# A spectral filter and a gated MLP on one core: W in six transfers, remainders on row halves, inverse tails as 32x32 blocks, and ten deferred tiles

## The chip, the cores and the metric

The kernel runs on one NeuronCore of a Trainium2 chip. The metric is device time in microseconds. The kernel before took 496.24 us (median of three runs, 496.06 to 496.64).

## What is computed

The input is one sequence of 2048 tokens with 576 features. A layer norm is filtered in two-dimensional frequency space and added to the input; a second layer norm goes through a gated MLP with 4608 hidden features and is added too.

```python
def _A_ref(x, w_r, w_i):
    X = jnp.fft.rfft2(x.astype(jnp.float32), axes=(-2, -1))
    X = X * (w_r + 1j * w_i)
    return jnp.fft.irfft2(X, s=(S, D), axes=(-2, -1)).astype(jnp.bfloat16)

def _B_ref(x, w_gate, w_up, w_down):
    return (_gelu(x @ w_gate) * (x @ w_up)) @ w_down

h = x + _A_ref(_layernorm(x), A_w_r, A_w_i)
h2 = h + _B_ref(_layernorm(h), B_w_gate, B_w_up, B_w_down)
```

`w_r` and `w_i` are 2048 x 289 each, in bf16. The transforms are done as matrix products with tables that lie in DRAM beside the inputs.

## The kernel before, in words

Sixteen tiles of 128 tokens each go through five stages. The orders of work in the first three are written out by hand in strings (`SEQ1`, `SEQF`, `SEQ`); each word is a step and its index. `Prog` turns reads and writes into semaphore waits, so each engine works through its own queue strictly in the order in which the steps were written.

**First stage (`SEQ1`, 0 to 20 us).** For each tile the statistics of the layer norm are taken on DVE (`B`) or on ACT (`S`, `Q`). Six groups of two or three tiles then get their scale (`v`, `q`, `c`), which is multiplied into the transform table `ATB` on GpSimd or DVE (`x..P`, `x..D`, result `ATS`); `n` negates half of the input on GpSimd. `M` runs the matmuls over tokens on PE (line 520), `k` runs matmuls on zeros while PE waits, and `E` brings results into `U` on ACT or DVE (line 529). `U` has five planes; plane 4 holds the 32 + 32 remainder features (256 to 287 and 544 to 575) on its rows 0 to 63. Rows 64 to 127 of it are set to zero once.

**Filter (`SEQF`, 20 to 52 us).** There are sixteen groups of frequencies. For each, `D` transforms over features (line 574: six matmuls with 128 rows, two of them on plane 4; evicted into `CUS` with a stride of two elements), `B` finishes the forward transform (line 584, into `YS`), `T` multiplies by W on DVE (line 594), `Z` adds the products into `ZS` and into the remainder `ZR` (lines 600 and 603), `V` starts the inverse over tokens (line 610, into `V`), and `R` does the same for the remainders of four groups at once (line 620), whose rows are then brought into `VR` in pieces of 32 partitions (line 565, four evictions a time). `VR` has a column for all sixteen groups, and all of it is zero but the pieces, so that the matmuls that read it can be 128 x 128.

**W.** `WS` holds three planes for each group: minus the imaginary part, the real part, the imaginary part. SyncE issues 36 transfers for it, after `VT` and before `DT`, `IT`, `DP`, `ITD` and `IDT`. The negative plane is made on GpSimd in sixteen steps (line 632), followed by the zeroing of `VR` (line 635). After these GpSimd issues the loads of the gate weights, and SyncE, after its tables, those of the up weights. The first third (slot 0) has its own place; slots 1 and 2 lie where W was.

**Inverse of the first eight tiles (`SEQ`, 52 to 65 us).** `I` is the inverse over features (line 684, six matmuls into two banks, the last of each three on `VR`), `N` the last step over tokens with the residual (lines 723 and 726), `s`, `m`, `r`, `q`, `c` and `n` the second layer norm, and `A`, `D` and `z` turn a tile on PE into `HT0` (line 777).

**MLP (65 us to the end).** There are four blocks of 512 tokens. For each, 36 chunks of 128 hidden features: eighteen matmuls with 64 rows (line 824, two row halves into two banks), GELU on ACT, a product on DVE. Then `down` (line 874): for each of the four tiles two halves of 36 matmuls. In the first block the inverse of tiles 8 to 15 (`def_i`, line 841, and `def_n`, line 855) is put into the matmuls of `down`, one in each half: `def_i` at its start, `def_n` before matmul 22. Tiles 4 to 7 are normed at chunks 15, 18, 21 and 24 of the first block and turned by DMA.

Matmuls in `def_i` before the change:

```python
for o in range(2):
    for t_ in range(2):
        for i, ch in enumerate((o, 2)):   # 128 x 144 each, ch == 2 reads VR
```

Of the kernel before, what the change touches and what calls it, by code (L numbers as in the profile page):

```python
# [10 lines left out]
KW = 288  # L11
HK = 144
NZ = 5
NVZ = 15
# [7 lines left out]
NPRE = 8  # L22
GROUPS = ((0, 2), (2, 4), (4, 7), (7, 10), (10, 13), (13, 16))
SEQ1 = """k14 B0 B1 v0 Q2 S2 B3 q0 v1 n0 n2 c0 q1 S4 x0D c1 M0 E1A B6 E0A Q4 B5 B7 x1P v2 E2D n1 B8 E3A E4A k104 M1 q2 c2 B9 Q10 E5A E7A n3 v3 S10 B12 E6A q3 c3 x2P B11 k202 M2 E9A x3P Q13 v4 E12A E8A q4 n4 B14 c4 B15 E10A E11A S13 E13D M3 E14A E15A v5 x4P E16D q5 E17A c5 E18A M4 n5 x5D E20D E19A E22D E21A M5 E23D E24A E25A E27A E26D E29A E28D""".split()
ACT_TILES = tuple(int(w[1:]) for w in SEQ1 if w[0] == "Q")
SEQF = """D0 D1 B0 D2 D3 T0 B1 D4 T1 B2 Z0 Z1 D5 T2 Z2 B3 D6 T3 B4 T4 D7 B5 Z4 D8 Z3 V0 B6 T5 Z5 T6 V1 B7 V3 Z6 T7 D9 R0 B8 D10 V2 Z7 D11 T8 B9 V6 B10 Z8 T9 R1 B11 V4 Z9 D12 D13 V5 T10 B12 T11 Z10 V7 B13 Z11 T12 T13 D14 R2 V9 D15 B14 V8 B15 Z12 V10 Z13 V13 V11 T14 Z14 V12 V14 T15a T15b Z15b Z15a R3 V15 R4""".split()
RENG = [['dve', 'dve', 'dve', 'dve'], ['dve', 'dve', 'dve', 'dve'], ['dve', 'dve', 'dve', 'act'], ['dve', 'dve', 'dve'], ['dve']]
QR = ((0, 2), (2, 4), (4, NPRE), (NPRE, 16))
SEQ = """I0 I1 N0 I2 s0 N1 I3 N2 m0 s1 I4 r0 q0 s2 N3 c0 m1 s3 n1 n0 r1 I5 q1 N4 I6 A1 c1 n3 A0 n2 N5 I7 D2 z3 N6 N7""".split()
# [11 lines left out]
def build_tables():  # L41
# [7 lines left out]
    T = {}  # L49
    n1 = np.arange(128)[:, None]  # L50
# [17 lines left out]
    I = I.reshape(4, 16, 2, 16, 128).transpose(1, 0, 2, 3, 4)  # L68
# [239 lines left out]
def _build(nc, A_x, A_w_r, A_w_i, B_w_gate, B_w_up, B_w_down, out):  # L308
# [16 lines left out]
    WS = sb.alloc("WS", [128, NG, 3, KW], BF16)  # L325
# [3 lines left out]
    VR = sb.alloc("VR", [128, NT, 2, NG, 8], BF16)  # L329
# [38 lines left out]
    FT = sb.alloc("FT", [128, 6, 2 * HK], BF16)  # L368
# [47 lines left out]
    x_load(0, 0, 2)  # L416
    x_load(1, 2, 4)
    atb_load(0, 0, 4)
    x_load(2, 4, 8)
    atb_load(1, 4, 8)  # L420
    x_load(3, 8, 12)
    x_load(4, 12, 16)
    atb_load(2, 8, 16)
    P.dma(SP, FT[:, :, :].rearrange("p a b -> p (a b)"), dram["FTAB"][:, :], "ft", w=["FT"])
    P.dma(SP, BT[:, :, :, :].rearrange("p a b c -> p (a b c)"), dram["BTAB"][:, :], "bt", w=["BT"])
    P.dma(SP, VT[:, :, :, :].rearrange("p a b c -> p (a b c)"), dram["VTAB"][:, :], "vt", w=["VT"])

    def w_loads(pl, hf, eng):
        g0, g1 = ((1, 9), (9, 16))[hf]
        src = (A_w_r, A_w_i)[pl]  # L430
        o = []
        for jj in range(4):
            o.append((WS[jj:64:4, g0:g1, 1 + pl, :], 1 + (16 * jj + g0) * K2, [[128 * K2, 16], [K2, g1 - g0], [1, K2 - 1]], jj))
            o.append((WS[64 + jj:128:4, g0:g1, 1 + pl, :], 1 + (64 + 16 * jj + 16 - g0) * K2, [[128 * K2, 16], [-K2, g1 - g0], [1, K2 - 1]], 4 + jj))
        if hf:
            for p0 in range(2):
                o.append((WS[64 * p0:64 * p0 + 64, 0, 1 + pl, :], 1 + 64 * p0 * K2, [[128 * K2, 16], [16 * K2, 4], [1, K2 - 1]], 8 + p0))
        return [lambda d=d, off=off, ap=ap, h=h: P.dma(eng, d, bass.AP(src.tensor, off, ap), f"w{pl}{hf}", w=[("W", hf, pl, h)]) for d, off, ap, h in o]

    for f in w_loads(1, 0, SP) + w_loads(1, 1, SP) + w_loads(0, 0, SP) + w_loads(0, 1, SP):  # L440
        f()
    GORD = list(range(1, NG)) + [0]
    wkeys = [[("W", hf, pl, h) for pl in range(2) for h in range(8 + 2 * hf)] for hf in range(2)]
# [6 lines left out]
    P.op(POOL, lambda g: g.memset(U[64:128, 4, :, :, :], 0.0), w=["Uz"])  # L450
# [56 lines left out]
    def a_mm(i):  # L507
        c0, c1 = GROUPS[i]
        for k in AORD:
            b = a_bank(i, k)  # L510
            for c in range(c0, c1):
                o = 128 * (c - c0)
                if k == 4:
                    parts = [(XO[:, c, 256 + 288 * h:288 + 288 * h], 32 * h, 32 * h + 32, True, True) for h in range(2)]
                else:
                    d0 = 128 * (k // 2)
                    x2 = XN[:, c, d0:d0 + 128] if k % 2 else XO[:, c, 288 + d0:416 + d0]
                    parts = [(XO[:, c, d0:d0 + 128], 0, 128, True, False), (x2, 0, 128, False, True)]
# [4 lines left out]
    def a_ev(n, eng):  # L523
        i, k = n // 5, AORD[n % 5]
        c0, c1 = GROUPS[i]
        n, b, w = c1 - c0, a_bank(i, k), 64 if k == 4 else 128
# [18 lines left out]
    P.alias([("XN", c) for c in range(NT)], [("V", g, c) for g in range(NG) for c in range(2)])  # L545
    uk = [[("U", i, k) for i in range(len(GROUPS))] + (["Uz"] if k == 4 else []) for k in range(5)]
# [4 lines left out]
    for t, w in enumerate(SEQF):  # L551
# [5 lines left out]
        elif k in "VR":  # L557
            b = min((6, 7) if ("D", LAST) not in FB else range(8), key=lambda b: used[b])
            used[b] = t + 1
        else:  # L560
            continue
# [6 lines left out]
    def st_D(i, eng=ACT):  # L568
        g = GORD[i]
        b0, s3 = FB["D", i], i % 3  # L570
        for o in range(2):
            b = b0 + o
            for m, us in enumerate((1 - o, 3 - o, 4) if o == 0 else (4, 1 - o, 3 - o)):
                P.op(PE, lambda t, b=b, m=m, us=us, o=o, g=g: t.matmul(bank(b, 0, 128, 0, 2 * HK), U[:, us, g, :, :], FT[:, 3 * o + (2 if us == 4 else us // 2), :], start=(m == 0), stop=(m == 2)),  # L574
                    r=uk[us] + ["FT"], w=[("PS", b)])
        ev(eng, CUS[:, s3, :, :].rearrange("p a (j r) -> p r a j", r=2), banks(b0, 2, 2 * HK).rearrange("p r (a j) -> p r a j", a=2),
           [("PS", b0), ("PS", b0 + 1)], [("CU", s3)])
# [10 lines left out]
    def st_T(i, q0=0, q1=KW, hs=(0, 1)):  # L588
        g, sl = GORD[i], i % 2
# [5 lines left out]
             r=[("Y", sl), ("Wn", i)] + wkeys[0 if 1 <= g < 9 else 1], w=[("T", sl, h) for h in hs])  # L595

    def st_Z(i, hs=(0, 1)):
# [3 lines left out]
        if 1 in hs:  # L601
            q, j = (i // 4 % 2, i % 4) if i < LAST else (0, 0)
# [3 lines left out]
    def st_V(i, b=6, eng=ACT):  # L606
        g, z3, sp_ = GORD[i], i % NZ, 1 if GORD[i] == 0 else 0
        for c in range(2):
            for zp in range(2):
                P.op(PE, lambda t, b=b, c=c, zp=zp, sp_=sp_, z3=z3: t.matmul(bank(b, 0, 128, 256 * c, 256 * c + 256), ZS[:, z3, zp, c:256:2], VT[:, sp_, zp, :],  # L610
                                                                            start=(zp == 0), stop=(zp == 1)), r=[("Z", z3), "VT"], w=[("PS", b)])
        for k0, k1, e in ((0, 4, eng),) if eng is not None else ((0, 2, ACT), (2, 4, ACT)):
            ev(e, V[:, :, k0:k1, g, :].rearrange("p n k e -> p k n e"), bank(b, 0, 128, 128 * k0, 128 * k1).rearrange("p (k n e) -> p k n e", k=k1 - k0, n=16),
               [("PS", b)], [("V", g, k) for k in range(k0 // 2, k1 // 2)])

    def st_R(q, engs, b=7):
        js = [i for i in range(4 * q, 4 * q + 4) if i < LAST] if q < 4 else [LAST]
        sp_, n = (1, 32) if q == 4 else (0, 32 * len(js))
        for zp in range(2):
            P.op(PE, lambda t, b=b, zp=zp, n=n, q=q, sp_=sp_: t.matmul(bank(b, 0, n, 0, 256), ZR[:, q % 2, zp, 0:n], VT[:, sp_, zp, :], start=(zp == 0), stop=(zp == 1)),  # L620
                 r=[("ZR", q % 2, j) for j in range(len(js))] + ["VT"], w=[("PS", b)])
        for j, i in enumerate(js):
            ev(engs[j], VR[32 * j:32 * j + 32, :, :, GORD[i], :].rearrange("p n k e -> p k n e"), bank(b, 32 * j, 32 * j + 32, 0, 256).rearrange("p (k n e) -> p k n e", k=2, n=16),
               [("PS", b), "Vz"], [("V", GORD[i], 2)])
# [6 lines left out]
    for i in range(NG):  # L631
        P.op(POOL, lambda v, g=GORD[i]: v.tensor_scalar(WS[:, g, 0, :], WS[:, g, 2, :], -1.0, 1.0, op0=ALU.mult, op1=ALU.mult),
             r=[k for k in wkeys[0 if 1 <= GORD[i] < 9 else 1] if k[2] == 1] + [("ATS", NT - 1)], w=[("Wn", i)])
        if i == NVZ:
            P.op(POOL, lambda g: g.memset(VR[:, :, :, :, :], 0.0), w=["Vz"])
    for w in SEQF:
        i = int(w[1:].rstrip("abc"))
        if w[0] == "D":
            st_D(i)
        elif w[0] == "B":  # L640
            st_B(i)
# [7 lines left out]
        elif w[0] == "V":  # L649
            st_V(i, FB["V", i], ACT if i < LAST else None)  # L650
# [21 lines left out]
    vk = [[("V", g, c) for g in range(NG)] for c in range(3)]  # L672
    vkeys = vk[0] + vk[1] + vk[2] + ["Vz"]
# [8 lines left out]
    def i_mm(c, h, i):  # L682
        b, kt = SLOT["I", c] + h, 2 * i + h
        P.op(PE, lambda t, b=b, h=h, i=i, kt=kt, c=c: t.matmul(bank(b, 0, 128, 0, KW), (V[:, c, kt, :, :] if kt < 4 else VR[:, c, kt - 4, :, :]), DT[:, 3 * h + i, 0:KW],  # L684
                                                              start=(i == 0), stop=(i == 2)), r=vk[i] + ["DT"], w=[("PS", b)])
# [262 lines left out]
```

## Time and profile before

| Stretch, us | what | PE busy, us | DVE busy, us | ACT busy, us | DMA share | GB/s |
|---|---|---|---|---|---|---|
| 0 to 20.0 | first stage | 16.86 | 15.37 | 15.23 | 0.81 | 248 |
| 20.0 to 27.3 | filter, before its first product | 7.04 | 0.60 | 5.52 | 0.43 | 91 |
| 27.3 to 52.4 | filter | 22.61 | 24.47 | 23.67 | 0.62 | 194 |
| 52.4 to 64.8 | inverse of eight tiles | 11.85 | 9.99 | 10.25 | 1.02 | 363 |
| 64.8 to 134.8 | chunks of block 0 | 70.00 | 27.31 | 26.92 | 0.42 | 135 |
| 134.8 to 176.2 | down of block 0 | 41.40 | 23.74 | 10.03 | 0.05 | 14 |
| 176.2 to 246.2 | chunks of block 1 | 70.00 | 27.00 | 23.71 | 0.18 | 50 |
| 246.2 to 281.6 | down of block 1 | 35.40 | 4.51 | 0.60 | 0.05 | 16 |

The profiled execution took 496.66 us; its span, from the first to the last instruction, is 494.9 us, and TensorE's granted clock was 1.00 throughout. Times in the table run from the start of the span. Busy time is the time in which at least one instruction of the engine was in flight; matmuls overlap, so a busy PE is not yet one at its limit, and starts of neighbouring instructions tell more than their durations. An instruction's duration on DVE or ACT overlaps the next one's by up to 0.2 us as well.

### The profile page before, as it was taken

Reading aid. Unit: us, or ns where it says so; the run is one execution under the profiler, and the core shown is the slowest. Engines: PE = TensorE matmul, PEld = TensorE weight load, DVE = VectorE, ACT = ScalarE, POOL = GpSimd, SP = SyncE. Lnnn points to the kernel's source line nnn. Section 1 sums busy time; section 2 is a strip of 40 time slices with the busy share of each in tenths; the row PEclk is TensorE's granted clock in tenths of the full one; section 3 lists DMA queues with packets and bytes.
Section 4 is the critical chain, followed back from the end, with each engine's and each line's share of the span. In section 5 each row is a group of like instructions: output and inputs, shape, how many; then the busy total and the mean of one; then the engine's idle time right before and its main releaser. Section 6 shows DMA issues by size and latency. Waiting matters only on the chain.

```text
span 494.9 us, 9880 instructions
## 1 busy us (share of the span) xinstructions
PE 486.1 (98%) x4338; PEld 288.1 (58%) x4338; DVE 192.4 (39%) x418; ACT 158.9 (32%) x300; POOL 34.6 (7%) x53
## 2 busy tenths in 40 slices
PE   7999999999999999999999999999999999999998
PEld 3767655555588854444477744444677544444775
DVE  6679743444365644433311144333211233333111
ACT  6989865232312243232300033232100132233000
POOL 5750701000000010000000000000000000000000
DMA  8666898411000062000000001000000000000000
GB/s 276 163 188 215 277 350 275 178 25 27 4 13 13 19 191 60 19 9 1 1 13 19 18 15 23 19 1 1 7 19 12 14 1 1 1 1 2 12 19 19
DMA packets 27164, 31.26 MB, mean 63 GB/s; under 512 B 11664, under 2 KB 20112, under 8 KB 27120
## 3 DMA queue, kind: packets, MB, share of 16 engines
q1 hardware_dynamic: 24224, 18.68, 13.0%
q0 software_dynamic: 2896, 11.95, 7.1%
q8 instruction: 34, 0.56, 0.5%
q14 instruction: 10, 0.08, 0.1%
HBM read 26.28 MB, written 2.36 MB: 58 GB/s over the span
## 4 chain that ended last, share of the span: by engine, by line
PE 88%; DVE 4%; issue 1%; ACT 0%; DVEq 0%
PE PS L824 57%; PE PS L874 29%; DVE TP L594 1%; DVE VR L565 1%; PE PS L841 1%; PE PS L684 1%; PE PS L723 1%; DVE ZS L600 1%; DVE XO L726 0%; PE PS L855 0%; DVE ZR L603 0%; PE PS L610 0%; DVE HN L757 0%; PE PS L777 0%; DVE TM L734 0%
## 5 line engine op out<-in xcount | busy, mean ns | idle before, releaser
L824 PE MATMUL PS<-HT,WG 64*128 64x512 bf16 x2106 | 228.5, 376 | 0.0
L824 PEld LDWEIGHTS PS<-HT,WG 64*128 64x128 bf16 x2106 | 107.3, 94 | 119.8 <-issue 1.0
L833 ACT ACTIVATE GL<-PS 128x512 bf16<-128x512 f32 x144 | 85.9, 597 | 257.3 <-PE PS L824 243.4
L834 DVE TENSOR_TENSOR AT<-GL,PS 128x512 bf16<-128x512 bf16 x144 | 98.9, 687 | 175.0 <-ACT GL L833 175.0
L874 PE MATMUL PS<-WD,AT 128*128 128x288 bf16 (+2 forms) x1152 | 144.3, 286 | 0.0
L874 PEld LDWEIGHTS PS<-WD,AT 128*128 128x128 bf16 x1152 | 110.8, 98 | 30.7 <-ACT GL L833 1.3
L877 DVE TENSOR_TENSOR OS<-PS,XO 128x288 bf16<-128x288 f32 (+2 forms) x32 | 14.6, 457 | 100.3 <-PE PS L874 100.3
L824 PE MATMUL PS<-HT,WGX 64*128 64x512 bf16 x486 | 53.4, 376 | 0.0
L824 PEld LDWEIGHTS PS<-HT,WGX 64*128 64x128 bf16 x486 | 23.7, 94 | 28.8
L714 ACT ACTIVATE JD<-XO 128x576 bf16<-128x576 bf16 x8 | 5.5, 683 | 28.5 <-DVE XO L858 28.5
L594 DVE TENSOR_TENSOR TP<-YS,WS 128x1152 bf16<-128x1152 bf16 (+2 forms) x17 | 11.8, 715 | 6.8 <-DMA WS<-in_A_w_r_dram 6.7
L574 PE MATMUL PS<-FT,U 128*128 128x288 bf16 x96 | 14.1, 286 | 0.1
L565 ACT ACTIVATE CUS<-PS 128x576 bf16<-128x576 f32 x16 | 13.5, 862 | 0.5 <-PE PS L574 0.4
L565 ACT ACTIVATE YS<-PS 128x576 bf16<-128x576 f32 x16 | 11.3, 705 | 2.3 <-DVE TP L594 2.2
L520 PE MATMUL PS<-ATS,XO 128*128 128x128 bf16 (+1 forms) x128 | 10.1, 221 | 1.7 <-POOL XN L534 1.1
L584 PE MATMUL PS<-CUS,BT 128*128 128x288 bf16 x64 | 10.5, 286 | 1.2 <-ACT YS L565 0.9
L464 DVE BATCH_NORM_STATS2 ST<-XO 128x6 f32<-128x288 bf16 x24 | 9.3, 438 | 4.5 <-DMA XO<-in_A_x_dram 4.5
L574 PEld LDWEIGHTS PS<-FT,U 128*128 128x128 bf16 x96 | 9.1, 98 | 2.9 <-ACT CUS L565 0.4
L520 PEld LDWEIGHTS PS<-ATS,XO 128*128 128x128 bf16 (+1 forms) x128 | 7.4, 97 | 4.7 <-POOL XN L534 1.6
L610 PE MATMUL PS<-VT,ZS 128*128 128x256 bf16 x64 | 9.0, 273 | 1.1 <-DVE VR L565 0.5
L565 ACT ACTIVATE V<-PS 128x512 bf16<-128x512 f32 (+1 forms) x17 | 10.0, 639 | 0.3 <-PE PS L610 0.2
L757 DVE TENSOR_SCALAR HN<-XO,TM,RS 128x576 bf16<-128x576 bf16 (+1 forms) x32 | 10.0, 361 | 0.0
(77 smaller groups left out, 215.0 us busy)
## 6 DMA issues: line engine op xcount, KB each, us to landing
WD<-in_B_w_down_dram POOLq DMA_DIRECT2D x9, 576.0 KB, 21.4
WG<-in_B_w_gate_dram POOLq DMA_DIRECT2D x4, 1152.0 KB, 9.7
WG<-in_B_w_up_dram SPq DMA_DIRECT2D x4, 1152.0 KB, 7.9
out_dram<-OS SPq DMA_DIRECT2D x30, 72.0 KB, 1.6
XO<-in_A_x_dram SPq DMA_DIRECT2D x3, 576.0 KB, 7.4
WGX<-in_B_w_gate_dram POOLq DMA_DIRECT2D x1, 1152.0 KB, 6.9
WGX<-in_B_w_up_dram SPq DMA_DIRECT2D x1, 1152.0 KB, 10.8
HT<-HN SPq DMA_TRANSPOSE x60, 2.4
```

The source lines that it names most:

```text
L464: P.op(DVE, lambda v, c=c, h=h: v.bn_stats(ST1[:, c, h, :], XO[:, c, 288 * h:288 * h + 288]), r=[("X", c)], w=[("ST1", c, h)])
L520: P.op(PE, lambda t, b=b, lhs=lhs, p0=p0, p1=p1, s=s, e=e, o=o, c=c: t.matmul(bank(b, p0, p1, o, o + 128), lhs, ATS[:, c, :], start=s, sto ...
L565: fn = (lambda v: v.tensor_copy(dst, src)) if eng == DVE else (lambda a: a.activation(dst, src, ACTF.Copy))
L574: P.op(PE, lambda t, b=b, m=m, us=us, o=o, g=g: t.matmul(bank(b, 0, 128, 0, 2 * HK), U[:, us, g, :, :], FT[:, 3 * o + (2 if us == 4 else u ...
L584: P.op(PE, lambda t, b=b, tb=tb, m=m, s3=s3, sp_=sp_: t.matmul(bank(b, 0, 128, 0, KW), BT[:, sp_, tb, :], CUS[:, s3, m, :], start=(m == 0) ...
L594: P.op(DVE, lambda v: v.tensor_tensor(TP[:, sl, :, :, q0:q1], y4, w4, op=ALU.mult), r=[("Y", sl), ("Wn", i)] + wkeys[0 if 1 <= g < 9 else ...
L757: P.op(eng, lambda v, c=c, hs=hs, o0=o0, o1=o1, x0=x0, x1=x1: v.tensor_scalar(HN[:, hs, o0:o1], XO[:, c, x0:x1], TM[:, 1, c:c + 1], RS2[:, ...
L824: op = P.op(PE, lambda t, h0=h0, kt=kt, wt=wt, b=b, s=(not second and j == 0), e=(second and j == n - 1): t.matmul(bank(b), wg_tile(slot)[ ...
L833: P.op(ACT, lambda a: a.activation(GL[:, s2, :], bank(b0), ACTF.Gelu_apprx_tanh), r=[("PS", b0)], w=[("GL", s2)])
L834: P.op(DVE, lambda v: v.tensor_tensor(AT[:, f, :], GL[:, s2, :], bank(b0 + 1), op=ALU.mult), r=[("GL", s2), ("PS", b0 + 1)], w=[("AT", f)])
L874: P.op(PE, lambda t, b=b, d0=d0, d1=d1, f=f, p=p: t.matmul(bank(b, 0, 128, 0, d1 - d0), AT[:, f, 128 * p:128 * p + 128], WD[:, f, d0:d1], ...
L877: P.op(DVE, lambda v, b=b, d0=d0, d1=d1, p=p, c=c: v.tensor_tensor(OS[:, p % 2, d0:d1], bank(b, 0, 128, 0, d1 - d0), XO[:, c, d0:d1], op=A ...
```

## The change

- **W in six transfers.** `w_load` replaces `w_loads`: per plane one transfer for rows 0 to 63, one for rows 64 to 127 (groups in reverse) and one for the row set of group 0. They stand before `VT` on SyncE. `WS` has one group more. The negative plane is made on DVE, four groups a step (`st_w`, words `w0` to `w3` in `SEQF`), and each `T` waits for all six transfers.
- **Remainders on two row halves.** Plane 4 of `U` now holds the remainder features twice, on rows 0 to 63 and 64 to 127 (four 32-column tails in `a_mm`). `st_D` runs the two remainder matmuls first, each on 64 rows, into two banks; the `CUS` eviction is written in another order of its dimensions. `FTAB` has five parts instead of six.
- **Tail inverse in diagonal blocks.** `VR` has four groups' room instead of sixteen and isn't zeroed; `st_R` evicts up to 128 partitions at once. What was one 128 x 128 matmul on `VR` in `i_mm` and `def_i` is four matmuls of 32 rows and 32 columns. The order of groups in `V` (`GSLOT`) and in the last table follows.
- **Ten tiles deferred.** `NPRE` is 6. Deferred tiles start every 28 matmuls of the first `down` (`DSTEP`), their last step comes 24 matmuls later (`DLAG`), and norms and turns of tiles 4 to 7 are put between them. `QR` has five groups of tiles.
- **Two first chunks by token parts.** Chunks 0 and 1 of block 0 run on tokens 0 to 383 first, then on 384 to 511.
- **Orders.** `SEQ1`, `SEQF`, `SEQ` are written anew; `DENG`, `BENG`, `VENG` and `RENG` put single evictions on DVE; group 15's `V` uses two banks and two engines.

```diff
-NPRE = 8
+NPRE = 6
+CUT = 384
-SEQF = """D0 D1 B0 D2 D3 T0 B1 D4 T1 B2 Z0 Z1 D5 T2 Z2 B3 D6 ...
+SEQF = """D0 D1 B0 B1 D2 D3 w0 D4 T0 B2 T1 D5 Z0 B3 Z1 T2 D6 ...
-QR = ((0, 2), (2, 4), (4, NPRE), (NPRE, 16))
-SEQ = """I0 I1 N0 I2 s0 N1 I3 N2 m0 s1 I4 r0 q0 s2 N3 c0 m1 s3 n1 n0 r1 I5 q1 N4 I6 A1 c1 n3 A0 n2 N5 I7 D2 z3 N6 N7""".split()
+QR = ((0, 2), (2, 3), (3, 4), (4, 8), (8, 16))
+DSTEP, DLAG = 28, 24
+SEQ = """I0 I1 N0 I2 N1 m0 s0 I3 N2 m1 s1 r0 s2 q0 N3 s3 m2 c0 r1 q1 n0 I4 n1 I5 c1 r2 n2 q2 z0 c2 n3 z1 A2 N4 N5 z3""".split()
...
-    VR = sb.alloc("VR", [128, NT, 2, NG, 8], BF16)
+    VR = sb.alloc("VR", [128, NT, 2, 4, 8], BF16)
...
+    def w_load(pl, part):
+        src = (A_w_r, A_w_i)[pl].tensor
+        if part == 0:
+            dst, ap = WS[0:64, 0:NG, 1 + pl, :], bass.AP(src, 1, [[128 * K2, 16], [K2, 64], [1, K2 - 1]])
+        elif part == 1:
+            dst, ap = WS[64:128, NG:0:-1, 1 + pl, :], bass.AP(src, 1 + 64 * K2, [[128 * K2, 16], [K2, 64], [1, K2 - 1]])
+        else:
+            dst, ap = WS[0:64, NG, 1 + pl, :], bass.AP(src, 1, [[128 * K2, 16], [16 * K2, 4], [1, K2 - 1]])
+        P.dma(SP, dst, ap, f"w{pl}{part}", w=[("W", pl, part)])
...
-    P.op(POOL, lambda g: g.memset(U[64:128, 4, :, :, :], 0.0), w=["Uz"])
...
-                    parts = [(XO[:, c, 256 + 288 * h:288 + 288 * h], 32 * h, 32 * h + 32, True, True) for h in range(2)]
+                    parts = [(XO[:, c, 256 + 288 * (h % 2):288 + 288 * (h % 2)], 32 * h, 32 * h + 32, True, True) for h in range(4)]
...
+        for m in range(3):
+            for o in range(2):
+                p0, p1 = (0, 128) if m else (64 * o, 64 * o + 64)
+                us, fs = (2 * m - 1 - o, 2 * o + m - 1) if m else (4, 4)
+                P.op(PE, lambda t, b=b0 + o, m=m, us=us, fs=fs, g=g, p0=p0, p1=p1: t.matmul(bank(b, 0, 128, 0, 2 * HK), U[p0:p1, us, g, :, :], FT[p0:p1, fs, :], start=(m == 0), stop=(m == 2)),
+                     r=uk[us] + ["FT"], w=[("PS", b0 + o)])
+        ev(eng, CUS[:, s3, :, :].rearrange("p a (j r) -> p a j r", r=2), banks(b0, 2, 2 * HK).rearrange("p r (a j) -> p a j r", a=2),
...
+    def st_w(i):
+        g0, g1 = 4 * i + 1, 4 * i + 5
+        P.op(DVE, lambda v: v.tensor_scalar(WS[:, g0:g1, 0, :], WS[:, g0:g1, 2, :], -1.0, None, op0=ALU.mult), r=wkeys[1], w=[("Wn", 4 * i + k) for k in range(4)])
...
-    for i in range(NG):
-        P.op(POOL, lambda v, g=GORD[i]: v.tensor_scalar(WS[:, g, 0, :], WS[:, g, 2, :], -1.0, 1.0, op0=ALU.mult, op1=ALU.mult),
...
+        for p0, p1 in [(0, 128)] if i < 2 else [(32 * j, 32 * j + 32) for j in range(4)]:
+            lhs = V[:, c, kt, :, :] if i < 2 else VR[p0:p1, c, h, :, :]
+            P.op(PE, lambda t, b=b, h=h, i=i, lhs=lhs, p0=p0, p1=p1: t.matmul(bank(b, p0, p1, 0, KW), lhs, DT[p0:p1, 3 * h + i, 0:KW],
...
+                    for p0, p1 in [(0, 128)] if ch < 2 else [(32 * j, 32 * j + 32) for j in range(4)]:
+                        lhs = V[:, c, 2 * ch + t_, :, :] if ch < 2 else VR[p0:p1, c, t_, :, :]
+                        P.op(PE, lambda t, o=o, t_=t_, i=i, lhs=lhs, p0=p0, p1=p1: t.matmul(bank(2 + o, p0, p1, HK * t_, HK * t_ + HK), lhs,
+                                                                                         DP[p0:p1, 2 * i + o, HK * t_:HK * t_ + HK], start=(i == 0), stop=(i == 1)),
...
+    for j, c in enumerate(range(NPRE, NT)):
+        defer(DSTEP * j, def_i, c)
+        defer(DSTEP * j + DLAG, def_n, c)
+    t2 = DSTEP * (8 - NPRE) + DLAG
+    defer(t2, ln2, 3)
+    for c in range(4, 8):
+        defer(t2 + 12 + DSTEP * (c - 4), turn, c)
...
+            if tb == 0 and f < 2:
+                if f == 0:
+                    for c0, c1 in ((0, CUT), (CUT, 512)):
+                        for a in range(4):
+                            gu_part(a % 2, a > 1, c0, c1)
```

## Prediction

> **What bounds the kernel now.** I read the page's first line and its shares, then the chain of waits in order of time, then the time lines of DVE, SyncE and PE by stage.
>
> ```profile
> PE 486.1 (98%) x4338; PEld 288.1 (58%) x4338; DVE 192.4 (39%) x418; ACT 158.9 (32%) x300; POOL 34.6 (7%) x53
> ...
> PE 88%; DVE 4%; issue 1%; ACT 0%; DVEq 0%
> ```
>
> The page says PE nearly everywhere. The chain (start, length, what, how many) says where not:
>
> ```profile
> 33.22 0.77 DVE TP L594
> ...
> 36.44 0.32 DVE VR L565
> ...
> 52.44 1.63 PE PS L684 x12
> ...
> 64.77 70.11 PE PS L824 x648
> 134.88 0.61 PE PS L841 x8
> 135.48 2.69 PE PS L874 x22
> 138.18 0.26 PE PS L855 x2
> ...
> 246.27 35.38 PE PS L874 x288
> ```
>
> Up to 52 us DVE sets the end: products (TP) and remainder evictions (VR). From 52.44 to 64.77 PE and DVE take turns on the inverse of eight tiles. From 64.77 on it is PE without a gap: a chunk pair costs 0.216 us (70.11/648 x 2), a 288-column matmul 0.123 us (35.38/288). The first down, 134.8 to 176.2, takes 41.36 us where a later one takes 35.38: eight deferred tiles, 0.75 us each, no gap. So later than 64.8 us a matmul more is time more.
>
> The filter starts late because SyncE hands out 36 transfers of W, 0.64 us apiece (first fence), and DVE waits 6.70 us for them (second fence):
>
> ```profile
> 6.76 12.71 SPq L218 DMA_DIRECT2D WS<-in_A_w_i_dram  x18
> 19.51 12.57 SPq L218 DMA_DIRECT2D WS<-in_A_w_r_dram  x18
> ```
>
> ```profile
> 27.26 1.43 DVE L594 TENSOR_TENSOR TP<-YS,WS 128x1152 bf16<-128x1152 bf16 x2 [6.70 <-DMA WS<-in_A_w_r_dram]
> ```
>
> The last view, PE's time line where the shape of the array tile changes, decides my forecast:
>
> ```profile
> 13.44 0.22 PE L520 MATMUL PS<-ATS,XN 128*128 128x128 bf16 x1
> 13.59 0.23 PE L520 MATMUL PS<-ATS,XO 128*32 128x128 bf16 x2
> ...
> 175.95 0.29 PE L874 MATMUL PS<-WD,AT 128*128 128x288 bf16 x1
> 176.16 0.39 PE L824 MATMUL PS<-HT,WG 64*128 64x512 bf16 x2
> ...
> 245.89 0.38 PE L824 MATMUL PS<-HT,WGX 64*128 64x512 bf16 x2
> 246.20 0.30 PE L874 MATMUL PS<-WD,AT 128*128 128x288 bf16 x1
> ```
>
> Start to start, 128*128 to 128*32 takes 0.150 us where two of one shape stand 0.056 apart; 128*128 to 64*128 takes 0.218 instead of 0.123; back, 0.308 instead of 0.213. Whatever the length of the matmul, a change of tile shape adds 0.095 us. The "x2" lines also show that matmuls on different tiles of one shape start together.
>
> [...]
>
> **The change part by part**, in us against the profiled execution (496.66, of which 494.9 is span and 1.8 lies around it).
>
> *First stage.* One more tile goes to DVE's statistics (about 0.8), three U evictions (0.5 each) and one scaling (0.4) leave it; ACT does three tiles instead of four (1.5 less) and three evictions more; x0 goes to GpSimd, whose 1.8 us memset of U goes. Four 32-column tails instead of two run side by side, so cost PE nothing more. Matmuls of the last three groups stand almost back to back (14.6 to 20.0), so I take only 0.3 earlier for D0: 19.7 (bounds 1.0 earlier, 0.5 later).
>
> *W in six transfers.* SyncE's W ends near 10 instead of 32; VT, DT, IT, DP, ITD, EYE and the first up-projection load follow at once. Ahead of W lie 3.45 MB; the first 20 us move 248 GB/s at a DMA share of 0.81, so 306 at full share: 11.3 us, from about 2, is 13.3. W is 2.36 MB; 20.0 to 27.3 shows 91 GB/s at 0.43, so 212: landed at 24.4. But GpSimd loses its 16 negations (6.9) and the VR memset (3.5), which held its gate load (1.3 MB) back to 30.1; it now issues it near 18, into W. At the 363 GB/s shown from 52.4 to 64.8 it is 3.6 us of DMA time, so W lands between 24.4 and 28.0; I take 26.5. The first product now needs all six transfers; before, the first half was enough. Four negations of 128x1152 enter DVE ahead of products, w0 within the wait; each 0.3 to 0.6 by the slope between the 128x64 (299 ns) and 128x576 (424 ns) rows, 0.4 taken.
>
> *Filter.* DVE worked 25.7 (27.26 to 52.95). Out: 15 VR evictions at 0.43, 6.5. In: three negations 1.2, D2 and B7 0.7 each, V6 and V14 0.6, half of V15 0.4, R3 0.4: 4.6. So 23.8, from 26.5 to 50.3. ACT loses one CUS, one YS, 2.5 V (3.2) and gains four 128x256 at 0.38 less one VR: 2.0 less; the new order of the CUS eviction is between 0.2 less each (the YS row, 705 ns against 862) and 0.4 more; I take 0.1 less. ACT is busy 29.2 from 20.0 to 52.4 (table by stage), so 25.7 now, and does not bind; at the dear end it would be 33.2 and end near 53.5. PE: D was 6 x 0.123 = 0.735; now the two row halves run together, 5 x 0.123, but go into and out of the 64-row shape: +0.19, so 0.80. Sum: 16 x (0.80 + 0.49 B + 0.436 V) + 1.1 R = 28.7, where before it was 27.6. From 19.7 that is 48.4 with no wait; before lost 4.9 to waits, and I leave 2.6 with W still late. The inverse starts at 51.0 instead of 52.44: **-1.4** (bounds -3.9 and, with ACT bound, +1.1).
>
> *Six tiles, blocks.* PE before: 8 x (0.73 I + 0.49 N) + 1.42 for turning four tiles = 11.2 in 12.33. Now each I has two sets of four 32x32 blocks. If blocks of a set run together, the set takes the time of the one matmul it replaces, plus two changes of shape: 4 x 0.095 = 0.38 a tile. 6 x (0.73 + 0.38 + 0.49) + 1.42 = 11.0; only one stall left, N3 behind I3's eviction, 0.4: 11.4. **-0.9**. Statistics of tile 2 apart from tile 3, and chunks 0 and 1 on tokens 0 to 383 first, hide the last turn's eviction (0.5); without that cover the stage would take 11.9.
>
> *Chunk parts.* 18 pairs of 384 columns and 18 of 128: 18 x (0.163 + 0.056) = 3.94 against 3.90, **+0.05**; up to +1.0 if two 64-row weight loads don't fit into 0.056.
>
> *First down.* Per tile def_i was 8 x 0.0616 = 0.49 and def_n 0.25. Now there are four sets of blocks in it: 8 changes, 0.76, and 0.04 of staggered starts. 10 x (0.49 + 0.80 + 0.25) = 15.4 against 5.97: **+9.4**. Of it two more tiles are 1.5, the changes 7.6. Norms and DMA turns of tiles 4 to 7 move from the first chunks into the down; SyncE and DVE have room there (DVE 23.7 busy of 41.4), and def_n, 24 matmuls or 2.9 us behind, is not late. The square root of these tiles leaves the GELU stage, where its two table loads were hidden anyway.
>
> Sum: -1.4 - 0.9 + 0.05 + 9.4 = **+7.2**. The profiled execution is 0.4 above the median shown, 496.24, so I forecast 496.24 + 7.2 = 503.4.
>
> **The rivals.**
> *A, blocks of a set queue* [...] Against: output quadrants differ, and 128*32 tiles with one bank start together. Per deferred tile 4 x 3 x 0.062 = 0.74, per early tile 2 x 3 x 0.123 = 0.74: +11.8, so 515.2.
> *B, faster: changes of shape around 32x32 blocks cost nothing*[...]. Then the inverse stage takes 9.4 (-2.9), the down +1.8, the filter, bound by DVE, -2.2: 493.0. The sign turns where a change costs under about 0.03 us. Against: all 19 changes of shape without a wait at them in this trace read 0.093 to 0.096, with 32-column weights too.
> *C, W no earlier*: [...] T0 at 28 or later, filter 0.0: 504.8; with ACT bound by the new eviction order, filter +1.1, 505.9. For it: the sharing worked out above; against: PE binds first.
>
> **How the numbers follow.** My forecast with C inside it: 0.78, own range 499 to 508.5 (the lower end has the filter at PE's sum without waits, the upper C plus a slow chunk split). A 0.10, B 0.10, anything else 0.02. Reaching up to A leaves out B and tails: 499 to 515.5. About 0.2% (1 us) is what a measurement of this kernel can tell from no change. Faster by that 0.11, within 0.02, slower 0.87.
>
> **What would show it.** Right: gaps near 0.15 us around 32*32 matmuls, four starting within some 10 ns; the first down near 51 us without other gaps; the first chunk near 62.5; first product between 24 and 28. Wrong: the down under 45 (B), a set spread over 0.25 us (A), or a filter ending before 48.

## The result, and the profile after

The changed kernel takes 512.31 us (median of four runs, 511.89 to 512.65), the kernel before beside it 496.43 us (496.06 to 496.64): a ratio of 1.032, 95% interval 1.0303 to 1.0338. The change costs 15.9 us where 7.2 were forecast. The profiled execution took 511.89 us, 510.1 of them span.

Stages by the start of their first instruction, in the two traces, in us:

| Stage | before | after | difference | forecast |
|---|---|---|---|---|
| first filter matmul (D0) | 19.98 | 20.11 | +0.1 | -0.3 |
| first product with W | 27.26 | 30.67 | +3.4 | -0.8 |
| inverse starts | 52.44 | 56.24 | +3.8 | -1.4 |
| inverse of the early tiles, length | 12.33 | 12.43 | +0.1 | -0.9 |
| chunks of block 0, length | 70.04 | 70.10 | +0.06 | +0.05 |
| first down, length | 41.36 | 52.09 | +10.7 | +9.4 |
| from there to the last matmul | 316.12 | 316.12 | 0 | 0 |

The start of the inverse and the four rows below it add up to 14.7 of the 15.2 us between the two spans. The other 0.5 lies behind the last matmul, where the code is the same; the traces of five of the seven experiments made from the changed kernel don't have it, so it is not the change's. So the miss sits in two places: mostly in the filter, which became longer instead of shorter, and less so in the inverse and the down.

The page of the changed kernel, its busy shares and the clock granted to PE in 40 slices (tenths of full speed):

```profile
PE 498.9 (98%) x4561; PEld 283.9 (56%) x4562; DVE 193.5 (38%) x422; ACT 153.3 (30%) x297; POOL 22.9 (4%) x36
...
PEclk9979999999999999999999999999999999999999
```

PE is busy 98% as before, but with 12.8 us more: the share hides it. The third slice, 25.5 to 38.3 us, is a place where the clock fell. The chain of waits in order of time (start, length, what, how many):

```profile
6.19 0.69 SPq L224
6.93 3.68 SPq L224
10.65 3.88 SPq L224
14.57 2.89 SPq L224
17.50 12.44 DMA WS<-in_A_w_i_dram
30.08 0.47 DVE WS L606
30.67 0.77 DVE TP L601
31.47 0.66 ACT YS L571
32.17 1.14 PE PS L591 x4
...
56.30 2.33 PE PS L695 x24
...
68.74 70.10 PE PS L835 x684
138.84 1.36 PE PS L853 x20
140.19 3.05 PE PS L905 x24
143.24 0.24 PE PS L867 x2
```

Read from the top: SyncE hands out W. The first transfer, 1024 rows, takes its queue 0.69 us, each of the next three, of the same size, 2.9 to 3.9 us. The fifth, of 64 rows only, is issued at 17.50 and lands at 29.95, 12.44 us later; only then the negation (L606), the first product (L601), and PE's next work at 32.17. In the down, `def_i` (L853) takes 1.36 us instead of 0.61.

PE's time line at the start of the down (start, length, how many in a row) shows what the blocks do:

```profile
138.77 0.24 PE L853 MATMUL PS<-DP,V 128*128 128x144 bf16 x1
138.93 0.24 PE L853 MATMUL PS<-DP,VR 32*32 32x144 bf16 x4
139.11 0.24 PE L853 MATMUL PS<-DP,V 128*128 128x144 bf16 x1
139.27 0.24 PE L853 MATMUL PS<-DP,VR 32*32 32x144 bf16 x4
```

Four blocks have together the length of one matmul (0.24): in the trace they start 3 ns apart, with different rows and in one PSUM bank. But from set to set it is 0.16 to 0.18 us, where two matmuls of one shape stand 0.062 apart.

### The profile page after: what moved, and what is told of

It reads as the page before. It is cut to its first block, busy times and chain, and to the rows that moved or that the text cites. A ratio compares the mean times of both kernels' runs of the same rounds, so it can differ in the third digit from the quotient of the medians.

```text
span 510.1 us, 10284 instructions
## 1 busy us (share of the span) xinstructions
PE 498.9 (98%) x4561; PEld 283.9 (56%) x4562; DVE 193.5 (38%) x422; ACT 153.3 (30%) x297; POOL 22.9 (4%) x36
## 4 chain that ended last, share of the span: by engine, by line
PE 91%; SPq 3%; DMA 2%; DVE 2%; ACT 1%; issue 0%; DVEq 0%
PE PS L835 55%; PE PS L905 27%; SPq L224 3%; DMA WS<-in_A_w_i_dram 2%; PE PS L853 2%; PE PS L581 2%; PE PS L621 1%; PE PS L591 1%; PE PS L695 1%; PE PS L734 1%; PE PS L867 1%; DVE HN L768 0%; DVE XO L737 0%; ACT L755 0%; PE PS L633 0%
## 5 line engine op out<-in xcount | busy, mean ns | idle before, releaser
L835 PE MATMUL PS<-HT,WG 64*128 64x512 bf16 (+2 forms) x2142 | 228.5, 372 | 0.0
L835 PEld LDWEIGHTS PS<-HT,WG 64*128 64x128 bf16 x2142 | 103.2, 94 | 123.7 <-issue 0.7
L725 ACT ACTIVATE JD<-XO 128x576 bf16<-128x576 bf16 x10 | 6.8, 682 | 39.1 <-DVE XO L870 39.1
L581 PE MATMUL PS<-FT,U 128*128 128x288 bf16 (+1 forms) x96 | 15.3, 308 | 0.0
L601 DVE TENSOR_TENSOR TP<-YS,WS 128x1152 bf16<-128x1152 bf16 (+2 forms) x17 | 11.8, 718 | 2.0 <-ACT YS L571 1.7
L860 DVE TENSOR_TENSOR QB<-PS,EB 128x288 f32<-128x288 f32 x20 | 8.2, 452 | 8.9 <-ACT EB L856 8.7
L571 ACT ACTIVATE YS<-PS 128x576 bf16<-128x576 f32 x15 | 9.7, 655 | 5.5 <-DVE TP L601 5.0
L581 PEld LDWEIGHTS PS<-FT,U 128*128 128x128 bf16 (+1 forms) x96 | 6.8, 99 | 7.5 <-issue 2.3
L571 ACT ACTIVATE CUS<-PS 128x576 bf16<-128x576 f32 x15 | 9.8, 652 | 3.8 <-PE PS L581 3.5
L870 DVE SCALAR_TENSOR_TENSOR XO<-PS,XO 128x576 bf16<-128x576 f32 x10 | 7.6, 757 | 8.1 <-PE PS L867 8.1
L591 PEld LDWEIGHTS PS<-CUS,BT 128*128 128x128 bf16 x64 | 6.4, 103 | 6.4 <-ACT YS L571 4.1
```

Source lines behind the costliest of these rows:

```text
L571: fn = (lambda v: v.tensor_copy(dst, src)) if eng == DVE else (lambda a: a.activation(dst, src, ACTF.Copy))
L581: P.op(PE, lambda t, b=b0 + o, m=m, us=us, fs=fs, g=g, p0=p0, p1=p1: t.matmul(bank(b, 0, 128, 0, 2 * HK), U[p0:p1, us, g, :, :], FT[p0:p1, ...
L591: P.op(PE, lambda t, b=b, tb=tb, m=m, s3=s3, sp_=sp_: t.matmul(bank(b, 0, 128, 0, KW), BT[:, sp_, tb, :], CUS[:, s3, m, :], start=(m == 0) ...
L601: P.op(DVE, lambda v: v.tensor_tensor(TP[:, sl, :, :, q0:q1], y4, w4, op=ALU.mult), r=[("Y", sl), ("Wn", i)] + wkeys[0] + wkeys[1], w=[("T ...
L835: op = P.op(PE, lambda t, h0=h0, kt=kt, wt=wt, b=b, s=(not second and j == 0), e=(second and j == n - 1): t.matmul(bank(b, 0, 128, c0, c1) ...
```

## The experiments

All compare with runs of the kernel before on the same chip. The stages that they were made for:

| Kernel | first product | inverse starts | inverse, length | first down, length | median, us | ratio (95% interval) |
|---|---|---|---|---|---|---|
| after | 30.67 | 56.24 | 12.43 | 52.09 | 512.31 | 1.032 (1.0303 to 1.0338) |
| e1_gate_held | 26.74 | 49.85 | 12.43 | 52.09 | 505.4 | 1.0181 (1.0166 to 1.0196) |
| e2_warm | 30.84 | 53.95 | 12.42 | 52.09 | 509.23 | 1.0259 (1.0244 to 1.0274) |
| e3_w_alone | 26.81 | 50.02 | 12.42 | 52.08 | 505.76 | 1.0186 (1.0169 to 1.0203) |
| e4_no_blocks | 30.57 | 55.16 | 10.97 | 46.32 | 503.15 | 1.0141 (1.0123 to 1.0159) |
| e5_grouped | 26.80 | 49.90 | 11.57 | 49.33 | 502.34 | 1.0115 (1.0099 to 1.013) |
| e6_d_full | 26.60 | 48.94 | 12.43 | 52.09 | 504.24 | 1.0155 (1.0139 to 1.017) |
| e9_grouped_turn_early | 26.64 | 49.91 | 11.56 | 48.23 | 500.54 | 1.0084 (1.007 to 1.0097) |
| e7_before_w_order | 23.51 | 52.36 | 12.36 | 41.36 | 496.9 | 1.0011 (1.0002 to 1.002) |
| e8_order_zero_early | 23.27 | 50.92 | 12.34 | 41.36 | 495.14 | 0.9974 (0.9964 to 0.9985) |
| e10_zero_in_wait | 23.16 | 51.19 | 12.33 | 41.36 | 495.44 | 0.9974 (0.9963 to 0.9985) |

### Who delays W: the gate load, or the tables

In the changed kernel GpSimd has nothing left to do after its part of the first stage and issues the first load of gate weights, 1.3 MB, at 17.1 us, while W is still being moved. e1 lets only this load wait for W:

```diff
-            P.dma(eng, tile[:, 4 * o:4 * o + 4, :], ..., f"wgu{o}{j}{slot}", w=[("WG", slot, o)])
+            P.dma(eng, tile[:, 4 * o:4 * o + 4, :], ..., f"wgu{o}{j}{slot}",
+                  r=wkeys[0] + wkeys[1] if (j, slot) == (0, 0) and o == 0 else [], w=[("WG", slot, o)])
```

> The changed kernel with GpSimd's first gate load held until all six W transfers have landed. Theory late W: the filter ends 5.3 us later than forecast because W lands at 29.95 instead of 26.5 and PE, idle for 4.1 us, restarts at half clock. If the gate load is what delays W, W lands near 26.5, PE idles under 1 us there, keeps its clock, and the inverse starts near 51.5 instead of 56.3: 507.5 in all. If the tables behind W on SyncE are the cause, W lands near 29 and little changes (511). Rival, the new filter order and its row halves are slow by themselves: even with an earlier W the filter still takes over 25 us from its first product.

e3 does the same and lets SyncE's tables (from `DT` on) and the first up load wait for W too:

```diff
-    P.dma(SP, DT[:, :, :].rearrange("p a b -> p (a b)"), dram["DTAB"][:, :], "dt", w=["DT"])
+    P.dma(SP, DT[:, :, :].rearrange("p a b -> p (a b)"), dram["DTAB"][:, :], "dt", r=wkeys[0] + wkeys[1], w=["DT"])
```

> As the run with the gate load held, and SyncE's tables from DT on wait for W too, so that after VT nothing but W is moved. Theory late W: W lands near 24.5 (2.4 MB at 212 GB/s behind 3.4 MB), the first product comes at 25, PE keeps its clock, the inverse starts near 50: 506 in all, and the difference to the run before is the tables' share. Rival, the six transfers are slow by themselves (each goes to 64 partitions): W lands at 28 or later although nothing else is moved.

GpSimd's and DVE's time lines, in the changed kernel first (in brackets the idle time before, and what ended it):

```profile
17.08 1.51 POOL L224 DMA_DIRECT2D WG<-in_B_w_gate_dram  x2
...
30.08 0.46 DVE L606 TENSOR_SCALAR WS<-WS 128x1152 bf16<-128x1152 bf16 x1 [5.17 <-DMA WS<-in_A_w_i_dram]
```

and with the gate load held (e1):

```profile
26.15 0.46 DVE L606 TENSOR_SCALAR WS<-WS 128x1152 bf16<-128x1152 bf16 x1 [1.45 <-DMA WS<-in_A_w_i_dram]
...
26.94 1.51 POOL L224 DMA_DIRECT2D WG<-in_B_w_gate_dram  x2 [9.93 <-DMA WS<-in_A_w_r_dram]
```

The same step of DVE starts 3.93 us earlier. No later stage got longer (the gate weights are first read at 62 us). The inverse starts 6.4 us sooner (at 49.85, where 51.5 was expected) and the kernel gains 6.9, more than the 3.9 by which W came sooner. Holding the tables as well (e3) adds nothing: the first product comes at 26.81, and 505.76 us lies within the interval of e1. So it is the gate load. W came in e3 neither at 24.5, as its theory had it, nor at 28 or later, as its rival had it.

### Why the filter also got longer: PE's clock

From the first product to the inverse the changed kernel takes 25.57 us, e1 23.11. The difference of 2.5 isn't W. In the changed kernel PE's last matmul before the gap ends at 28.39, and PE stands for 3.78 us, to 32.17. The clock granted to PE is 1.00 up to 30.8 us, within the gap, 0.50 from there to 37.6, and then 1.00 again. e2 leaves W late and gives PE 26 matmuls without use in that gap:

```diff
         elif w[0] == "D":
+            if i == 6:
+                idle_ft(26, FB["D", i])
             st_D(i, DENG[i])
```

> The changed kernel with 26 matmuls more (3.2 us, results overwritten) ahead of D6, in the time in which PE has nothing to do while W is missing. Nothing else changes; W still lands near 30. Theory cold PE: PE idles about 0.9 us instead of 4.1, its granted clock stays whole, 288-column matmuls after it stand 0.123 apart instead of 0.24, and the inverse starts near 53 instead of 56.3: 509 in all. Rival, the filter is slow because of its order or because DVE sets its pace from the first product on: the start of the inverse stays within 0.7 of 56.3.

The busy time by stretch (PE, PEld, DVE, ACT, POOL, then the granted clock, the DMA share and GB/s), in the changed kernel:

```profile
28.00:32.10 4.10, 0.39 (x4) 0.08 (x1) 1.89 (x4) 0.63 (x2) 0.00 (x0) 0.84 1.05 357
32.10:39.00 6.90, 6.83 (x35) 3.93 (x36) 5.32 (x16) 5.27 (x11) 0.00 (x0) 0.60 0.68 231
39.00:56.00 17.00, 17.00 (x142) 12.31 (x140) 14.97 (x39) 15.84 (x31) 0.98 (x2) 1.00 0.03 3
```

and with the gap filled (e2):

```profile
28.00:32.10 4.10, 4.10 (x34) 2.84 (x31) 1.71 (x3) 0.46 (x1) 0.00 (x0) 1.00 1.04 362
32.10:39.00 6.90, 6.71 (x55) 4.75 (x55) 6.90 (x19) 6.74 (x14) 0.00 (x0) 1.00 0.65 218
```

After the gap the clock is 0.60 over 6.9 us, and PE, busy throughout, gets 35 matmuls done in them instead of 55. With the gap filled the filter takes 23.11 us although W is as late as ever, 2.46 less; the inverse starts 2.3 sooner and the kernel gains 3.1. The late W thus cost 6.4 at the inverse: 3.9 itself, 2.5 in the clock behind it.

In the changed kernel the clock thus fell 2.4 us after PE's last matmul had ended and came back 5.5 us after PE had begun again. Such a gap does not always cost as much. In e4, described below, this part of the kernel is unchanged, W is as late and PE stands for 4.03 us:

```profile
32.10:39.00 6.90, 6.90 (x44) 4.11 (x45) 5.91 (x17) 5.92 (x11) 0.00 (x0) 0.75 0.67 218
```

There the clock is 0.50 from 32.3 to 35.7 us only, half as long, and the filter takes 24.59 us, 1.5 more than in e1 and not 2.5. Of e4's four executions the three like this one have a mean clock of 0.997 and spans of 501.2 to 501.4 us; the fourth has 0.993, as all four of the changed kernel have, and 503.2.

### What the blocks cost, and what comes of it when they go

e4 replaces each set of four blocks by one 128 x 128 matmul on a plane of `V`: no changes of shape, the rest as it was. It leaves the remainder features out of the inverse.

```diff
-        for p0, p1 in [(0, 128)] if i < 2 else [(32 * j, 32 * j + 32) for j in range(4)]:
-            lhs = V[:, c, kt, :, :] if i < 2 else VR[p0:p1, c, h, :, :]
+        for p0, p1 in [(0, 128)]:
+            lhs = V[:, c, kt, :, :] if i < 2 else V[:, c, h, :, :]
...
(the same in def_i)
```

> The changed kernel with each set of four 32x32 blocks replaced by one 128x128 matmul of the same 288 or 144 columns, on a plane of V instead of VR; it leaves the remainders out of the inverse and puts other data there, so only its time counts. Theory: the first down takes 10 x (0.49 + 0.25) + 35.4 = 42.8 plus the 0.5 in which PE waits for a square root's table, instead of 52.1, and the inverse of six tiles 12.4 - 6 x 0.42 = 9.9: 501 in all. Rival, the deferred tiles cost more because of their new places among the matmuls of down: the down stays over 46.

e5 starts from e1 and keeps the computation, but puts the sets of blocks next to each other, so that half of the changes of shape go: two for an early tile instead of four, four for a deferred one instead of eight.

```diff
-        for o in range(2):
-            for t_ in range(2):
-                for i, ch in enumerate((o, 2)):
+        for t_ in range(2):
+            for i, o in ((0, 0), (0, 1), (1, 0), (1, 1)):
+                for ch in ((o, 2)[i],):
...
         for h in range(2):
-            for i in range(3):
+            for i in range(2):
                 i_mm(c, h, i)
+        for h in range(2):
+            i_mm(c, h, 2)
```

> The changed kernel with the gate load held (e1) and the matmuls of the inverse in another order: in each deferred tile the blocks of two sets stand together (4 changes of tile shape instead of 8), in each early tile likewise (2 instead of 4). The same matmuls, no more and no fewer. Theory, the price is per change of shape, 0.107 with the slower start of the matmul behind it: the first down falls by 10 x 4 x 0.107 = 4.3 from 52.1 to 47.8, the inverse of six tiles by 12 x 0.107 = 1.3 from 12.4 to 11.1, 500 in all. If the transposes of tiles 4 to 7, which SyncE issues at 1.3 us each, come too late for the second block, PE waits up to 1 us at the end of the down. Rival, the price is per block: nothing changes (505.4).

PE's time line of a grouped deferred tile:

```profile
131.57 0.30 PE L856 MATMUL PS<-DP,V 128*128 128x144 bf16 x2
131.80 0.30 PE L856 MATMUL PS<-DP,VR 32*32 32x144 bf16 x8
132.04 0.30 PE L856 MATMUL PS<-DP,V 128*128 128x144 bf16 x2
132.27 0.30 PE L856 MATMUL PS<-DP,VR 32*32 32x144 bf16 x8
132.50 1.28 PE L908 MATMUL PS<-WD,AT 128*128 128x288 bf16 x9
```

Both runs missed their forecasts for the down: 49.33 us in e5 instead of 47.8, 46.32 in e4 instead of 43.3, which is where e4's rival (the new places among the matmuls of `down`) put it. The tile itself does what the theory says: 0.93 us instead of 1.35, so a change is (1.35 - 0.93)/4 = 0.105. That is 4.2 us over ten tiles, but the down became only 2.8 shorter in e5 and 5.8 in e4, where some 8.5 of changes went. PE's waits grew: by 1.5 in e5, which is the whole difference there, and by 2.1 in e4, which leaves 0.6 open. So e4's rival is right in part. PE's waits during the down (for what, us in total, times, longest), in e4:

```profile
PE PS L867 <- DVE YB L863: 1.3, 1, 1.3
PE PS L835 <- DMA HT<-HN: 1.3, 1, 1.3
```

In the changed kernel only the first of them is there, with 0.5. Both waits belong to what the change moved from the chunks into the down. The first: the square root of tiles 4 to 7 brings a table load of ScalarE in front of `EB`, which `def_n` needs. ScalarE and PE in the changed kernel:

```profile
155.17 1.28 ACT L755 ACT_TABLE_LOAD   x1
...
156.47 0.30 ACT L755 ACTIVATE RS<-RS,EPT 128x4 f32<-128x4 f32 x1
156.67 0.39 ACT L856 ACTIVATE EB<-PS 128x288 f32<-128x288 f32 x1
...
158.83 0.42 PE L867 MATMUL PS<-YB,ITD 128*128 128x288 bf16 x2 [0.49 <-DVE YB L863]
```

The second: SyncE's twenty transposing transfers take some 1.3 us each (ten of them 13.14 in a row, up to 186.9), and a shorter down reaches the chunks of block 1 before they are through. e9 makes e5's statistics and turns of tiles 4 to 7 due 26 places sooner:

```diff
-    t2 = DSTEP * (8 - NPRE) + DLAG
+    t2 = DSTEP * (7 - NPRE) + DLAG + 2
```

> e5_grouped with the statistics and the turns of tiles 4 to 7 due 26 places (some 3.2 us) sooner in the first down: directly behind tile 7's deferred part. If SyncE's 20 transposing transfers end too late for the second block in e5_grouped (PE waited 1.34 us at 179.6), that wait goes: the first down 48.0 to 48.3 us instead of 49.33, the kernel 501.0 to 501.4 instead of 502.34. Rival (the wait there has another cause, or comes back at the square root's table or at DVE): 49.3 and 502.3.

The down takes 48.23 us, 1.1 less, and of PE's waits there only the first is left:

```profile
PE PS L870 <- DVE YB L866: 0.9, 1, 0.9
```

The kernel gains 1.8 us on e5, of which 1.1 are this wait; the two were measured at different times, and where the other 0.7 are from stays open.

### The row halves of D

e6 starts from e1 and lets the two remainder matmuls of each `D` run on all 128 rows again. Rows of the other half are then added in, so its data aren't the filter's.

```diff
-                p0, p1 = (0, 128) if m else (64 * o, 64 * o + 64)
+                p0, p1 = 0, 128
```

> e1 with the two remainder matmuls of each D over all 128 rows of plane 4 instead of 64 rows each; it thereby adds the other half's product to each, so its data are not the filter's and only its time counts. Theory: D is 6 x 0.123 = 0.74 instead of 0.123 x 5 + 2 x 0.107 = 0.83, so the row halves cost 16 x 0.09 = 1.5 of PE time in the filter; PE binds there, and the inverse starts 1.0 to 1.5 earlier than in e1 (49.85): 504.2 in all. Rival, DVE sets the filter's pace: the start of the inverse stays within 0.3.

The inverse starts at 48.94 instead of 49.85, and the kernel takes 504.24 instead of 505.4 us. The intervals of the two ratios overlap a little (up to 1.017, and from 1.0166), so the medians alone don't decide it; but the four runs that keep the row halves and have W early start the inverse within 0.17 us of one another (49.85 to 50.02), and 0.9 is clear of that. It is a little less than the 1.0 to 1.5 expected: two matmuls side by side with two changes of shape are dearer than one after the other in one shape (0.82 to 0.83 us a `D` against 0.73 in e6, 41.65 to 42.38).

### Does the kernel before gain from an earlier W at all?

e7 is the kernel before with one line changed: SyncE issues the first halves of both planes ahead of the second ones.

```diff
-    for f in w_loads(1, 0, SP) + w_loads(1, 1, SP) + w_loads(0, 0, SP) + w_loads(0, 1, SP):
+    for f in w_loads(1, 0, SP) + w_loads(0, 0, SP) + w_loads(1, 1, SP) + w_loads(0, 1, SP):
```

> The kernel before with one line changed: SyncE issues the first half of both planes of W before the second half of either, so that the first product needs 16 transfers issued instead of 26. Theory, the filter before is held back by its first product at 27.26: that moves to about 23.4, where YS is ready, the inverse starts 2 to 3.5 earlier (49 to 50.5 instead of 52.44) and all of it reaches the end: 493 to 494.5. Rival, DVE then waits for the second half at the ninth product instead, or PE binds: the inverse starts within 0.7 of 52.44 and the time stays 496.4.

The first product comes 3.75 us sooner, and nothing is gained: the inverse stays within 0.1 us of where it was, as the rival had it, if for another reason. DVE's time line further on:

```profile
33.68 0.75 DVE L594 TENSOR_TENSOR TP<-YS,WS 128x1152 bf16<-128x1152 bf16 x1
...
36.27 1.72 DVE L565 CAST VR<-PS 32x256 bf16<-32x256 f32 x4 [0.61 <-POOL VR L635]
```

GpSimd's later negations now wait 4.3 us for W's second half, the zeroing of `VR` behind them comes late, DVE's evictions into `VR` wait 0.61 us for it, and PE waits 2.0 us for DVE. e8 has the zeroing earlier, by the one number that places it:

```diff
-NVZ = 15
+NVZ = 8
```

> The kernel before with two small edits: its 36 weight transfers in the order of the first halves of both planes first (as in e7_before_w_order), and GpSimd's zeroing of VR set after the eighth negation instead of the fifteenth, so that it lies in GpSimd's 4.3 us of waiting for the second half. My theory of e7 (the first product came 3.75 us sooner, at 23.51, and the gain was lost because the zeros came late: DVE's VR evictions stood behind the memset and PE behind DVE): the first product at 23.5, the inverse at 49 to 50.5 instead of 52.4, the kernel 494.0 to 495.5 (ratio 0.995 to 0.998). Rival 1 (DVE is the bound: its small sums take 0.41 us instead of 0.18 while GpSimd negates, and it needs all of its time): the inverse at 51.5 to 52.4 and 496 to 496.9. Rival 2 (PE's work sets the filter's length and e7 lost it at PE's start): the inverse at 23.5 + 23.1 = 46.6 and about 491.

The inverse starts at 50.92, a little later than expected; the kernel takes 495.14 us, 0.26% less than before (0.15 to 0.36%). But the zeroing stood one negation too late to fall into GpSimd's wait, which e10 mends:

```diff
-NVZ = 8
+NVZ = 7
```

> e8_order_zero_early with the zeroing of VR one place sooner: behind the eighth negation. In e8 it stood behind the ninth, which itself waits for the second half of W, so that the 3.5 us of zeroing lay at 28.0 to 31.5, behind GpSimd's wait of 4.7 us instead of in it, and the negations ended at 36.2. My theory (in e8 DVE and ScalarE are busy 91 and 96% of the filter from 23 to 51, so that the filter's length is their work, and only what GpSimd's negations add to DVE's small sums and PE's 0.69 us at 35.9 behind them is still to be had): the inverse at 50.3 to 50.9 (50.92 in e8), the kernel 494.5 to 495.1. Rival (GpSimd's late negations are what holds the filter): the inverse at 48.5 to 49.5 and 492.8 to 493.8.

No further gain: 51.19, 495.44 us, with the same ratio as e8, though the negations now end 3.3 us sooner; so it isn't GpSimd that holds the filter. e8 and e10 are the two versions here that are faster than the kernel before. What is left is in the busy time by stretch, in e8:

```profile
23.00:30.00 7.00, 7.00 (x59) 5.59 (x58) 5.12 (x12) 6.89 (x12) 3.00 (x2) 1.00 0.34 79
30.00:36.00 6.00, 6.00 (x53) 4.92 (x51) 5.81 (x14) 6.00 (x12) 5.42 (x8) 1.00 0.68 208
36.00:43.00 7.00, 6.11 (x51) 4.70 (x50) 6.82 (x18) 6.34 (x11) 1.70 (x3) 1.00 1.02 355
43.00:51.00 8.00, 7.14 (x58) 5.09 (x57) 7.80 (x23) 7.72 (x16) 1.58 (x3) 1.00 0.37 105
```

From 30 us on DVE (third figure) is busy 20.4 of 21 us, ScalarE (fourth) 20.1. With W on time the old filter is near the limit of these two engines, and that is probably why most of the earlier start is lost; no run took work from them alone. The changed one takes 23.1 us from the first product (e1) where e8 takes 27.65. It has five `VR` evictions, one of them on DVE, in place of fifteen on DVE, at some 0.42 us each, but also other orders of work, and no run separates these. As a whole the new filter does bring something once W is early: e1, e3, e5, e6 and e9 start the inverse sooner than any form of the kernel before. The down takes it back.

## Why the prediction was right or wrong

The direction was right, and the reason given for it too: changes of tile shape in the first down are the largest single cost (80 of them at 0.107 us, 8.6 us). The size was wrong by 8.7 us, and the step that failed is the filter, above all the landing of W in it: the start of the inverse was forecast at -1.4 and came at +3.8, which is 5.2 of the 8.7. The inverse (1.0) and the down (1.3) were mis-sized; the rest lies behind the last matmul and between profiled runs and medians.

- **W landing at 26.5, "between 24.4 and 28.0": failed.** It landed at 29.95. Two terms were wrong. One is the base of 24.4: without the gate load W is there at about 26.1 (e1), and with the tables held back too no sooner (e3). SyncE's queue was busy with W until 20.7 and not 10, but that need not be the cause: in e3 the DMA engines were full all the same from 14 to 24 us (share 1.15 to 1.23) and moved 198 to 208 GB/s, near the 212 reckoned with; only the last 2 us were emptier. Where the 1.7 us come from stays open. And the gate load's 3.6 us, worked out correctly (3.9 measured), were added only in part: I took a value inside the two bounds, as if the two loads might not meet. e1 shows that they do: with the gate load out of the way W is there 3.9 us sooner.
- **No term for PE's clock: the larger omission in kind.** The forecast left PE 2.6 us of waits and priced them at their length. The wait of 3.8 us that came also had PE's clock at 0.50 for the work behind it, to 37.6 us, which cost 2.5 us (e2). With W early and the clock whole (e1) the filter came better than forecast: 23.11 us from the first product where DVE's work was reckoned at 23.8, and the inverse at 49.85 instead of 51.0.
- **D's row halves: right.** Five matmuls and two changes at 0.80 were forecast against 0.735; the chain has 0.82 to 0.83, and e6 gives back 0.9 at the inverse.
- **Inverse of six tiles, 11.4: mis-sized, 12.43.** PE's work was about as forecast (0.107 a change instead of 0.095 adds 0.3), but I left only one stall of 0.4. The chain goes from 62.57 to 67.04 through DVE's residual and norm steps, so a part of what PE is spared only becomes waiting: e5 takes away twelve changes, 1.28 us, and gains 0.86.
- **Chunk parts, +0.05: right**, +0.06.
- **First down, +9.4: mis-sized, +10.73.** A deferred tile takes 5.04 us from one to the next with 28 matmuls of `down` between them (3.44), so 1.60 instead of 1.54: a change costs (1.60 - 0.74)/8 = 0.107. Ten tiles make 16.0 against 5.97 before; the table load's wait adds 0.5; 0.2 stay without a name. "The square root leaves the GELU stage, where its two table loads were hidden anyway" was true (1.28 us each, at 82.28 and 83.89 in the trace of before, and no wait of PE in the chunks of block 0), but not that it is hidden where it goes to.
- **Turns moved into the down, SyncE has room: right.** The last of the twenty is issued by 186.9 us, and PE goes on with block 1 at 190.85. e4, e5 and e9 show the room used up as soon as the down is shorter.
- **The rivals.** A (blocks of a set queue) is out: with different rows, different output partitions and one PSUM bank they start 3 ns apart. B (changes are free) is out at 0.107. Its inverse of 9.4 us also doesn't follow from its own terms, 6 x (0.73 + 0.49) + 1.42 + 0.4 = 9.1, which changes nothing here. C had the right cause, the gate load in W's way (3.9 us, e1), but stopped at "28 or later" and a filter no longer than before.

## What to carry to other kernels

When a change frees an engine that issues loads, write down when its next load goes out, and add the whole of its bytes to whatever is then in flight: one dependency on that load was worth 6.9 us here. Price an idle stretch of PE like the two here (3.78 and 4.03 us) not at its length alone but with the slow clock behind it, here 2.5 and 1.5 us, or fill it with matmuls. Splitting a matmul into blocks of another tile shape is worth it only if the blocks save more than two changes, here 0.107 us each; put all blocks of one shape next to each other, and look at what becomes the last wait before you count the gain.

## What was not expected of the hardware

- Small steps of DVE got slower beside one kind of GpSimd's work and not beside another. In e8 a sum into `ZR` takes 0.18 us while GpSimd zeroes `VR` (28.0 to 31.5) and 0.40 while it negates (31.6 to 36.2); GpSimd's own negations take 0.50 us each while DVE waits for W (the kernel before) and on average 0.66 (a row of seven, e8) to 0.74 (a row of eight, e10) beside its work. What makes the difference no run shows. DVE and GpSimd in e8:

```profile
28.13 0.18 DVE L603 TENSOR_TENSOR ZR<-TP 128x64 bf16<-128x64 bf16 x1
...
32.30 0.40 DVE L603 TENSOR_TENSOR ZR<-TP 128x64 bf16<-128x64 bf16 x1
```

```profile
27.99 3.52 POOL L635 MEMSET VR<- 128x4096 bf16 x1
31.59 4.65 POOL L632 TENSOR_SCALAR WS<-WS 128x288 bf16<-128x288 bf16 x7
```

- Fewer transfers did not mean as much less time on SyncE's queue. Of the six, the first, 1024 rows of 576 bytes, takes 0.69 us to issue, the next three of the same size 2.9 to 3.9 us, and the fifth, 64 rows, 2.57 us; so it isn't the rows of the transfer being issued that set it, and what does, no run shows. The 36 smaller ones before took 25.3 us in all, 0.70 each on average, so the six saved SyncE 11 us and not the 22 of the forecast.
- Two sets of four 32x32 blocks in a row (e5) take as long as two matmuls of the same columns, 0.30 us for both: the blocks themselves cost nothing extra, their change of shape does (0.105 us).
